# Decay attention and its FFN on one core: f loaded first, two scale loads in program order, FFN units dealt evenly per step

## The chip, the cores and the metric

The kernel runs on one core of one Trainium2 chip. The metric is the device time of one execution in microseconds; shown is the median of several runs. The profile is one more execution, taken by the hardware profiler. The engines are called by what they do: TensorE (PE in the profile, its weight loads PEld), VectorE (DVE), ScalarE (ACT), GpSimd (POOL) and SyncE (SP), which only issues DMAs.

## The reference

Eight batches of eight heads, 576 positions, head size 64. The attention has a decay: the logs of f are summed along the sequence, and the difference of the sums is added to the scores. The heads' outputs, side by side, are 4608 tokens of 512 numbers, and go through a feed-forward network (FFN) of 2048 hidden units. The weights come as 64-bit floats.

```python
scores = scale * np.matmul(q, k.transpose(0, 1, 3, 2))
log_f = np.log(np.clip(f, 0.0001, 1.0))
cum = np.cumsum(log_f, axis=-1)
decay = cum[:, :, :, None] - cum[:, :, None, :]
scores = np.where(causal, -1000000000.0, scores + decay)
attn = softmax(scores)                    # written out in the reference
x = (attn @ v).transpose(0, 2, 1, 3).reshape(B * S, H * D)
h = x @ w_in
g = np.where(h >= 1, h, np.where(h <= -1, 0.0, (h + 1) ** 2 / 4))
out = g @ w_out
```

## The kernel before

**Jobs and rounds.** The attention works in jobs. A job is a pair of heads (`hp`, 0 to 3) of a batch over a range of row tiles `r0` to `r1` (128 rows each; the fifth tile has 64 rows). Batch 0 is cut in two: jobs 0-3 do row tiles 0 and 1, jobs 4-7 tiles 2 to 4. From batch 1 on a job does all five: jobs 8-11 are batch 1, 12-15 batch 2, and so on to job 35. Four jobs with the same rows are a round; when its last pair has its values, the tokens of these rows are complete and the FFN can use them.

**Steps.** The loop over `p` (L737) writes out the work job by job as a list of steps: one per row tile (scores of the next tile, softmax of this one), and as second entry `finish`, which multiplies the weights of job `p - 1` with its values and, after the last pair, sets `tokens`. So the tokens of a round become known in the second step of the next round's first job. Scores use matrix products in 32 bits up to job 11 and split 16-bit ones from job 12; values are split from job 8.

**The FFN** is dealt in units. A unit is one chunk of 256 tokens by one of eight blocks of 256 hidden units: `moe_front` (first product, L637, into PSUM tile `ph`; then ScalarE and VectorE, L646 to L651, through tile `u`) and `moe_back` (second product, L665), which is written out one unit later. There are 18 chunks, so 144 units. Chunk 0 is done in three groups of blocks, since the weights come late: `weight_load` and `weight_split` read and convert the eight blocks during jobs 1 to 6 (`CONVERT`), mostly on VectorE.

**How units are dealt.** At the head of each job the loop works out a `quota` from the units that are ready by then: a share of one in four, three, two or one, by how many jobs are left until the next change of `tokens`. After each step it writes out units until the job's share for that step is reached. What is not dealt by the end of the loop follows after it.

**Scales.** The 16-bit splits need powers of two that fit the largest value of a batch. `value_scale(b)` (L244, L245) and `query_scale(b)` (L268, L269) read a batch's v, or q and k, once more, in 288 KB pieces into tiles `vm` (two of them), take maxima on VectorE, and `across` (L119, L129) brings them together over partitions with TensorE in PSUM tile `s`, of which there is one and which the scores use too. `value_scale(b)` is called while the job before batch `b` runs, `query_scale(b)` three jobs ahead, in the first row step: for batch 2 in job 9. The loads of these are issued by GpSimd, which also makes the decay rows (L474, L478) that the scores are added to.

**Order.** The program is traced in the order of the loop, and a scheduler then sets the order on each engine by running the program through a model of the chip: an instruction that is ready goes, the earlier in the program first. So an instruction that waits for nothing but a free tile can be placed far ahead of the place where the loop wrote it. On the chip each engine then works off its queue in that order. `decay_sums` (L140) loads f, takes logs and running sums, and writes them to DRAM, from where `load_decay` (L372) spreads a head's sums over all partitions.

Of the kernel before, what the change touches and what calls it, by code (L numbers as in the profile page):

```python
# [30 lines left out]
NQK = 12  # L31
# [14 lines left out]
def kernel(  # L46
# [20 lines left out]
    nc = tc.nc  # L67

    B, H, S, D = q.shape
# [67 lines left out]
    cum_d = dram.tile([B * H, S], F32, name="cum_d")  # L137
    cq8 = const.tile([P, NT5, B * H], F32, name="cq8")

    def decay_sums():  # L140
        fl = early
        nb = B * H
        nc.sync.dma_start(fl[0:nb, 0:S], f.rearrange("b h s -> (b h) s"))
        nc.vector.tensor_scalar(
            out=fl[0:nb, 0:S], in0=fl[0:nb, 0:S], scalar1=1e-4, scalar2=1.0, op0=ALU.max, op1=ALU.min
        )
        nc.scalar.activation(fl[0:nb, S:2 * S], fl[0:nb, 0:S], AF.Ln)
        nc.gpsimd.memset(fl[0:nb, 3 * S:4 * S], 0.0)
        cum = fl[0:nb, 2 * S:3 * S]
        nc.vector.tensor_tensor_scan(  # L150
            out=cum, data0=fl[0:nb, S:2 * S], data1=fl[0:nb, 3 * S:4 * S], initial=0.0, op0=ALU.add, op1=ALU.add
        )
        nc.sync.dma_start(cum_d, cum)
        pt = ps1.tile([P, 1024], F32, name="big")
        twice = fl[0:nb, 0:P]
        nc.vector.tensor_copy(
            twice.rearrange("p (a b) -> p a b", a=2), cum[:, FULL:S].unsqueeze(1).broadcast_to([nb, 2, 64])
        )
        for t in range(NT5):
            nc.tensor.transpose(  # L160
                pt[:, nb * t:nb * t + nb], cum[:, P * t:P * t + P] if t < LAST else twice, ident[0:nb, 0:nb]
            )
        nc.vector.tensor_scalar(
            out=cq8.rearrange("p t n -> p (t n)"), in0=pt[:, 0:NT5 * nb], scalar1=8.0, scalar2=None, op0=ALU.mult
        )
# [70 lines left out]
    def value_scale(b):  # L236
        m4 = tiny.tile([P, NPAIR], F32, name="m4", bufs=2)
        for i in range(NPAIR):
            if b:
                st = two.tile([P, S], F32, name="vm")  # L240
            else:
                st = stage[:, i * S:(i + 1) * S]
            part = v[b, 2 * i:2 * i + 2].rearrange("h s d -> (h s d)").rearrange("(p n) -> p n", p=P)
            (nc.gpsimd if b else nc.sync).dma_start(st, part)  # L244
            nc.vector.tensor_reduce(  # L245
                out=m4[:, i:i + 1], in_=st, axis=AX.X, op=ALU.max, apply_absolute_value=True
            )
        m1 = tiny.tile([P, 1], F32, name="m1", bufs=2)
        nc.vector.tensor_reduce(out=m1, in_=m4, axis=AX.X, op=ALU.max)
        m = mv[:, b:b + 1]  # L250
        across(m, m1)
        if b:
            nc.vector.tensor_tensor(out=m, in0=m, in1=mv[:, b - 1:b], op=ALU.max)
        scale_of(sv[:, b:b + 1], pv[:, b:b + 1], m)
# [6 lines left out]
    def query_scale(b):  # L261

        ms = tiny.tile([P, 2, NPAIR], F32, name="m8", bufs=2)
        for j, src in enumerate((q, k)):
            for i in range(NPAIR):
                st = two.tile([P, S], F32, name="vm")
                part = src[b, 2 * i:2 * i + 2].rearrange("h s d -> (h s d)").rearrange("(p n) -> p n", p=P)
                nc.gpsimd.dma_start(st, part)  # L268
                nc.vector.tensor_reduce(  # L269
                    out=ms[:, j, i:i + 1], in_=st, axis=AX.X, op=ALU.max, apply_absolute_value=True  # L270
                )
        m2 = tiny.tile([P, 2], F32, name="m2q", bufs=2)
        nc.vector.tensor_reduce(out=m2, in_=ms, axis=AX.X, op=ALU.max)
        mk = tiny.tile([P, 2], F32, name="mk", bufs=2)
        across(mk, m2)
        sc = sqk[:, :, b]
        scale_of(sc, mk, mk)
        nc.vector.tensor_scalar(
            out=nsig[:, b:b + 1], in0=sc[:, 0:1], scalar1=sc[:, 1:2], scalar2=-8.0, op0=ALU.mult, op1=ALU.mult
        )  # L280
        nc.vector.reciprocal(nalpha[:, b:b + 1], nsig[:, b:b + 1])
        nc.vector.tensor_scalar(
            out=cqs[b % 2], in0=cq8[:, :, b * H:(b + 1) * H], scalar1=nsig[:, b:b + 1], scalar2=-0.125,
            op0=ALU.mult, op1=ALU.mult,
        )
# [412 lines left out]
    done = 0  # L698
    tokens = 0
    nload = 0  # L700
    nw = 0

    def ready():
# [33 lines left out]
    for p in range(njobs + 1):  # L737
# [26 lines left out]
        if p > 0:  # L764
            wp = pairs[p - 1]

            def finish():
                nonlocal tokens
                (early_values if wp.p < NPE else values)(wp, xs[wp.b])
                if wp.hp == NPAIR - 1:  # L770
                    if wp.b and wp.r0 == 0:
                        join_scales(wp.b - 1)
                    tokens = wp.b * S + wp.s1

            steps.insert(1, finish)
        load_weights(LOADS.get(p, 0))
        blocks = CONVERT.get(p, 0)
        quota = -(-ready() // (NPAIR - (p + NPAIR - 1) % NPAIR))
        before, wbefore = done, nw
        for i, st in enumerate(steps):  # L780
            st()
            while nw - wbefore < blocks * (i + 1) // len(steps):
                weight_step()
            while ready() and done - before < quota * (i + 1) // len(steps):
                if units[done] not in bsc and nw < NB:
                    break
                moe_unit(*units[done])
# [36 lines left out]
```

## Time and profile before

| what | value |
|---|---|
| median of 3 runs | 1199.87 us (1199.61 to 1200.08) |
| the profiled execution's own time | 1195.69 us |
| its span, first to last instruction | 1193.9 us |
| mean granted TensorE clock | 0.951 |
| busy in the span: TensorE, VectorE, ScalarE, GpSimd | 89%, 68%, 65%, 40% |

How to read the rows: a row of instructions gives start, duration, engine, line of the kernel, operation, tiles written and read, and in brackets how long the engine had been idle before and what ended that. A row of the stages gives the stretch, its length, each engine's busy time and number of instructions (x), the mean granted clock of TensorE (PEclk), the share of the DMA engines' time and the rate. A row of waits gives who waited for whom, then the total in us, the number of waits and the longest. In a group's row stand shapes, count, busy time and the mean ns of one; an issue's row ends with the size in KB and the median us to landing. SPq and POOL rows of DMA_DIRECT2D are issues of transfers.

### The profile page before, as it was taken

Reading aid. Unit: us, or ns where it says so; the run is one execution under the profiler, and the core shown is the slowest. Engines: PE = TensorE matmul, PEld = TensorE weight load, DVE = VectorE, ACT = ScalarE, POOL = GpSimd, SP = SyncE. Lnnn points to the kernel's source line nnn. Section 1 sums busy time; section 2 is a strip of 40 time slices with the busy share of each in tenths; the row PEclk is TensorE's granted clock in tenths of the full one; section 3 lists DMA queues with packets and bytes.
Section 4 is the critical chain, followed back from the end, with each engine's and each line's share of the span. In section 5 each row is a group of like instructions: output and inputs, shape, how many; then the busy total and the mean of one; then the engine's idle time right before and its main releaser. Section 6 shows DMA issues by size and latency. Waiting matters only on the chain. (4 is left out here: it accounts for less than half of the span.)

```text
span 1193.9 us, 24608 instructions
## 1 busy us (share of the span) xinstructions
PE 1064.8 (89%) x8871; PEld 681.6 (57%) x8871; DVE 806.8 (68%) x2140; ACT 770.4 (65%) x1599; POOL 476.1 (40%) x811
## 2 busy tenths in 40 slices
PE   2566766998689899999999999999999999999998
PEld 1334443655356556655666665565566666677665
DVE  5979878777778777768656666777767866522222
ACT  2756555758567767777667666786777776644443
POOL 3588643534464544544432232454434444000000
PEclk9767888999789999999999999999999999999999
DMA  8797744689989977867665555777767773300000
GB/s 269 220 296 210 216 138 143 134 192 162 181 159 201 188 132 161 153 137 147 123 115 103 108 111 116 149 157 139 141 129 146 128 130 66 74 19 2 19 18 18
DMA packets 392537, 162.60 MB, mean 136 GB/s; under 512 B 370016, under 2 KB 371040, under 8 KB 392416
## 3 DMA queue, kind: packets, MB, share of 16 engines
q1 hardware_dynamic: 377312, 115.03, 49.4%
q0 software_dynamic: 9920, 36.58, 10.8%
q10 hardware_dynamic: 5184, 9.44, 2.3%
q8 instruction: 69, 1.13, 0.4%
q14 instruction: 52, 0.43, 0.1%
HBM read 89.80 MB, written 9.58 MB: 83 GB/s over the span
## 5 line engine op out<-in xcount | busy, mean ns | idle before, releaser
L637 PE MATMUL ph<-x,place 128*128 128x256 f16 (+3 forms) x4608 | 430.3, 248 | 10.1 <-DVE u L648 8.0
L665 PE MATMUL po<-place,g 128*128 128x512 f16 x1728 | 412.8, 382 | 4.1 <-ACT g L650 3.9
L637 PEld LDWEIGHTS <-place 128*128 128x128 f16 x4608 | 355.4, 99 | 85.4 <-issue 29.2
L474 POOL TENSOR_SCALAR sdr<-ck,nsig,cqs 128x128 f32<-128x128 f32 (+1 forms) x192 | 154.3, 808 | 297.7 <-DVE pr L575 278.5
L665 PEld LDWEIGHTS <-g 128*128 128x128 f16 x1728 | 162.3, 98 | 176.9 <-issue 8.3
L560 ACT ACTIVATE sdr<-sdr,nm 128x128 f32<-128x128 f32 (+1 forms) x240 | 132.6, 553 | 75.8 <-DVE nm L556 75.1
L648 DVE SCALAR_TENSOR_TENSOR u<-ph,z,u 128x512 f32<-128x512 f32 x136 | 101.5, 746 | 107.0 <-ACT u L647 106.7
L646 ACT ACTIVATE u<-ph,z 128x512 f32<-128x512 f32 x136 | 104.4, 768 | 80.0 <-PE ph L637 78.1
L650 ACT ACTIVATE g<-u,z 128x512 f16<-128x512 f32 x136 | 97.8, 719 | 71.0 <-DVE u L648 67.1
L575 DVE SCALAR_TENSOR_TENSOR pr<-sdr,rc,pr 128x128 f16<-128x128 f32 (+1 forms) x224 | 116.3, 555 | 39.9 <-ACT pr L574 37.7
L651 DVE SCALAR_TENSOR_TENSOR g<-u,z,g 128x512 f16<-128x512 f32 x136 | 104.2, 766 | 48.1 <-ACT g L650 47.6
L574 ACT ACTIVATE pr<-sdr,rc 128x128 f16<-128x128 f32 (+1 forms) x224 | 112.6, 550 | 18.9 <-ACT sdr L560 14.3
L556 DVE CUSTOM_DVE_ANT_0 sdr<-s,sdr,nalpha 128x128 f32<-128x128 f32 (+1 forms) x192 | 98.4, 546 | 26.5 <-PE s L466 16.2
L466 PE MATMUL s<-qkT 64*128 64x128 f16 (+5 forms) x704 | 88.3, 347 | 26.7 <-DVE nm L556 23.9
L595 PE MATMUL big<-pT,vs 128*64 128x64 f16 (+3 forms) x1008 | 83.8, 291 | 18.6 <-DMA pT<-pr 10.8
L647 ACT ACTIVATE u<-u 128x512 f32<-128x512 f32 x144 | 89.8, 624 | 2.5
L478 POOL TENSOR_SCALAR_AFFINE_SELECT sdr<-sdr 128x128 f32<-128x128 f32 x240 | 85.0, 363 | 7.8
L595 PEld LDWEIGHTS <-vs 128*64 128x64 f16 x1008 | 53.1, 113 | 51.6 <-issue 33.2
L474 POOL TENSOR_SCALAR sd<-ck,nsig,cqs 64x576 f32<-64x576 f32 x48 | 47.0, 980 | 78.9 <-DMA ck<-cum_d 60.5
L466 PEld LDWEIGHTS <-qkT 64*128 64x128 f16 (+1 forms) x864 | 32.8, 99 | 59.7 <-issue 46.1
L390 DVE SCALAR_TENSOR_TENSOR qs<-qk,sqk,qs 128x640 f16<-128x640 f32 x48 | 42.4, 910 | 30.8 <-ACT qs L389 30.8
L389 ACT ACTIVATE qs<-qk,sqk 128x640 f16<-128x640 f32 x48 | 37.3, 820 | 38.8 <-DMA qkT<-qs 33.2
(163 smaller groups left out, 1140.3 us busy)
## 6 DMA issues: line engine op xcount, KB each, us to landing
ck<-cum_d POOLq DMA_DIRECT2D x48, 288.0 KB, 4.5
out_dram<-ot ACTq DMA_DIRECT2D x36, 256.0 KB, 3.5
qk<-in_k_dram SPq DMA_DIRECT2D x64, 128.0 KB, 3.1
vm<-in_v_dram POOLq DMA_DIRECT2D x28, 288.0 KB, 3.5
v<-in_v_dram SPq DMA_DIRECT2D x56, 128.0 KB, 3.0
qk<-in_q_dram SPq DMA_DIRECT2D x56, 128.0 KB, 2.8
vm<-in_q_dram POOLq DMA_DIRECT2D x24, 288.0 KB, 3.4
vm<-in_k_dram POOLq DMA_DIRECT2D x24, 288.0 KB, 3.4
```

The source lines that it names most:

```text
L466: nc.tensor.matmul(outs[h][:, c0:c1], lhsT=x[rows], rhs=y[rows, c0:c1], start=(i == 0), stop=(i == len(terms) - 1),)
L474: nc.gpsimd.tensor_scalar(out=sd[p0:p1, 0:wid], in0=w.ck[h][p0:p1, 0:wid], scalar1=w.nsig if w.p < NQK else w.nsig[p0:p1], scalar2=w.cqs[p ...
L556: nc.vector.tensor_tensor_reduce(out=a, in0=sp, in1=a, scale=w.nalpha, scalar=BIG, op0=ALU.add, op1=ALU.min, accum_out=nm[:, i:i + 1],)
L560: nc.scalar.activation(a, a, AF.Exp, bias=nm[:, i:i + 1], scale=-1.0, accum_out=sm[:, i:i + 1])
L574: nc.scalar.activation(pr[:, :, 0, i, :], a, AF.Copy, scale=rc[:, i:i + 1])
L575: nc.vector.scalar_tensor_tensor(out=pr[:, :, 1, i, :], in0=a, scalar=rc[:, i:i + 1], in1=pr[:, :, 0, i, :], op0=ALU.mult, op1=ALU.subtract,)
L595: nc.tensor.matmul(av[64 * h:64 * h + 64, at + s0:at + s1], lhsT=w.vs[:, vl, h, t, :], rhs=w.pT[:, t, pl, h, s0:s1], start=(t == 0 and pi ...
L637: nc.tensor.matmul(ph[:, fi, a0:a1], lhsT=wi[fb][:, wl, t, fi * P:(fi + 1) * P], rhs=xs[b][:, t, xl, s0:s0 + a1 - a0], start=(fi == 0 and ...
L646: nc.scalar.activation(u, h, AF.Relu, scale=z.u[:, i:i + 1], bias=z.h[:, i:i + 1])
L648: nc.vector.scalar_tensor_tensor(out=u, in0=h, scalar=z.t[:, i:i + 1], in1=u, op0=ALU.max, op1=ALU.min)
L651: nc.vector.scalar_tensor_tensor(out=g[:, 1], in0=u, scalar=z.r[:, i:i + 1], in1=g[:, 0], op0=ALU.mult, op1=ALU.subtract)
L665: nc.tensor.matmul(po[ch][i], lhsT=g[:, gl, fi * TC + i * P:fi * TC + (i + 1) * P], rhs=wo[fb][:, wl, fi, :], start=(first and fi == 0 and ...
```

## The change

There are three edits. The load of f is traced ahead of everything else on its queue, before the first pair's q and k; it stood inside `decay_sums`, behind them. The loads of `value_scale(1)` (four) and of `query_scale(2)` (eight) are passed to `keep_in_program_order`, which puts each behind the instruction traced before it on GpSimd's queue; the loads of the other batches are left as they were. And `quota` is replaced by a plan: when a round is complete, `finish` notes the units done, the units ready, the number of steps so far and the number of steps until the next round is complete; after each step, units are due in proportion to the steps since then.

```diff
+    nc.sync.dma_start(early[0:B * H, 0:S], f.rearrange("b h s -> (b h) s"))
     def decay_sums():
         fl = early
         nb = B * H
-        nc.sync.dma_start(fl[0:nb, 0:S], f.rearrange("b h s -> (b h) s"))
...
-            (nc.gpsimd if b else nc.sync).dma_start(st, part)
+            load = (nc.gpsimd if b else nc.sync).dma_start(st, part)
+            if b == 1:
+                tc.keep_in_program_order(load)
...
-                nc.gpsimd.dma_start(st, part)
+                load = nc.gpsimd.dma_start(st, part)
+                if 4 * (b + 1) == NQK:
+                    tc.keep_in_program_order(load)
...
+    plan = [0, 0, 0, 1]
+    step_no = 0
...
                     tokens = wp.b * S + wp.s1
+                    to_come = sum(r1 - r0 + 1 for _, _, r0, r1 in jobs[p:p + NPAIR])
+                    plan[:] = [done, ready(), step_no, max(1, to_come)]
...
-        quota = -(-ready() // (NPAIR - (p + NPAIR - 1) % NPAIR))
-        before, wbefore = done, nw
+        wbefore = nw
         for i, st in enumerate(steps):
             st()
             while nw - wbefore < blocks * (i + 1) // len(steps):
                 weight_step()
-            while ready() and done - before < quota * (i + 1) // len(steps):
+            step_no += 1
+            due = plan[0] + -(-plan[1] * (step_no - plan[2]) // plan[3])
+            while ready() and done < due:
```

## The prediction

> **What bounds the kernel now.** I read the page's head and its slices first, then cut the span into stages with the windows view, because the mean over the span says nothing here.
>
> ```profile
> span 1193.9 us, 24608 instructions
> PEclk9767888999789999999999999999999999999999
> ```
>
> The slices are 29.8 us each: the granted TensorE clock is below full speed in the first ten, then it is full. The stages below are cut where ScalarE first evacuates the values of jobs 3, 7, 11, 15 and 35, the last job of each round (here the first and the last of these five instructions):
>
> ```profile
> 88.77 0.45 ACT L536 ACTIVATE x<-po,sv 128x256 f16<-128x256 f32 x1
> 1042.09 0.65 ACT L604 ACTIVATE x<-big 128x576 f16<-128x576 f32 x1 [4.41 <-PE big L595]
> ```
>
> Busy time of all engines by stage:
>
> ```profile
> core 0: us, PE busy (x) PEld busy (x) DVE busy (x) ACT busy (x) POOL busy (x), PEclk, DMA share, GB/s
> 0.00:88.80 88.80, 41.35 (x175) 26.41 (x177) 64.20 (x186) 46.61 (x125) 52.71 (x89) 0.79 0.86 261
> 88.80:222.20 133.40, 95.04 (x566) 62.38 (x567) 108.91 (x313) 76.83 (x180) 76.98 (x116) 0.83 0.60 177
> 222.20:329.00 106.80, 91.90 (x669) 54.43 (x668) 81.15 (x233) 71.95 (x157) 46.83 (x88) 0.92 0.86 168
> 329.00:437.50 108.50, 95.38 (x906) 62.22 (x904) 83.38 (x221) 74.36 (x158) 54.59 (x98) 0.94 0.87 175
> 437.50:1042.10 604.60, 593.86 (x5371) 375.73 (x5371) 426.33 (x1134) 435.62 (x893) 245.03 (x423) 1.00 0.67 127
> 1042.10:1194.00 151.90, 147.22 (x1194) 100.41 (x1192) 42.81 (x57) 65.03 (x93) 0.00 (x0) 1.00 0.04 15
> ```
>
> From 437.5 us on TensorE is the bound: it idles 10.7 us in 604.6, and 4.7 in the last 151.9. Before that it idles 47.5, 38.4, 14.9 and 13.1 us. A unit moved from one late place to another is worth nothing; a unit moved from the end into an idle place early is worth up to its whole TensorE time.
>
> How many FFN units ran in each stage is read from the back half's matmuls (L665, twelve to a unit):
>
> ```profile
> 0.00:88.80 88.80, 0.00 (x0) 0.79 0.86 261
> 88.80:222.20 133.40, 17.03 (x60) 0.83 0.60 177
> 222.20:329.00 106.80, 32.17 (x132) 0.92 0.86 168
> 329.00:437.50 108.50, 31.05 (x133) 0.94 0.87 175
> 437.50:1042.10 604.60, 250.09 (x1056) 1.00 0.67 127
> 1042.10:1194.00 151.90, 82.44 (x348) 1.00 0.04 15
> ```
>
> That is 0, 5, 11, 11, 88 and 29 units. In the last stage nothing but units is left, so a unit costs 151.9 / 29 = 5.24 us of TensorE.
>
> **The dealing, part by part.** Before, tokens that become ready in job 4, 8, 12 ... were dealt over the next four jobs, so jobs 5-8 had 2 units each, 9-12 2, 13-16 4, 17-20 4, 21-24 6, 25-36 4, and 24 were left. The new plan starts inside the step that completes the round and counts its steps (16 for the cut batch, 24 for the others): jobs 4-7 get 2 each, 8-11 2, 12-15 4, 16-19 4, 20-23 6, 24-35 4, and 24 are left. Everything moves one job earlier. With the back half one unit late, the stages would have 0, 7, 8, 16, 88 and 25 units: changes of 0, +2, -3, +5, 0, -4. The gate on converted weights holds nothing up: three blocks are split by the end of job 3 and eight by the end of job 6, ahead of units 0 and 6 in jobs 4 and 7. The stages are costed one by one.
>
> Last stage: -4 x 5.24 = **-21.0 us**. It has no other work, so nothing can give that back inside it.
>
> Stage 437-1042: the same 88 units, **0**.
>
> Stage 329-437: five more units are 26.2 us of TensorE. It has 13.1 us of idle, and at the granted 0.94 some 0.06 x 95 = 5.7 us are lost to the clock. If both were filled the cost would be 26.2 - 18.8 = 7; if neither, 26. TensorE is 88% busy in it, nearer to filled; I take half the sum of both idle kinds plus a little for order, **+13** (7 to 26).
>
> Stage 222-329: three units fewer, -15.7 if TensorE set its length throughout. Against that stands the scale of batch 2, below, which I put at +11: **-5** net (-16 to +20).
>
> Stage 88-222: two units more. TensorE has 38.4 us idle; VectorE pays two instructions of a unit:
>
> ```profile
> L651 DVE SCALAR_TENSOR_TENSOR g<-u,z,g 128x512 f16<-128x512 f32 x136 | 104.2, 766 | 48.1 <-ACT g L650 47.6
> L648 DVE SCALAR_TENSOR_TENSOR u<-ph,z,u 128x512 f32<-128x512 f32 x136 | 101.5, 746 | 107.0 <-ACT u L647 106.7
> ```
>
> so 2 x 1.5 = 3 us on an engine that is 82% busy there. The units also take turns in PSUM tile `ph` and tile `u` with the row turning and the weight split. I take +2 for both, at most +8.
>
> **The loads in program order.** Today the scale loads run far ahead of their place, since they need only a free `vm` tile. Reduces of such loads (L269 queries and keys, L245 values) in the two early stages:
>
> ```profile
> 0.00:88.80 88.80, 4.41 (x6) 0.79 0.86 261
> 88.80:222.20 133.40, 19.33 (x26) 0.83 0.60 177
> 88.80:222.20 133.40, 11.99 (x16) 0.83 0.60 177
> ```
>
> The twelve pinned loads belong to batch 1's values (asked for in job 7) and batch 2's queries and keys (job 9). Would the loads behind them simply run ahead in their place? The trace says that tiles of one name are handed out in program order: batch 1's value maximum was ready early, and its transpose, which needs PSUM tile `s`, still came at its place in the program, though `s` had stood free in between:
>
> ```profile
> 22.65 0.15 DVE L249 TENSOR_REDUCE m<-m 128x1 f32<-128x4 f32 x1
> 198.67 0.37 PE L119 MATMUL s<-ident,m 128*1 128x128 f32 x1 [6.27 <-DVE nm L556]
> ```
>
> So all 76 queue behind job 7. In the first stage go four reduces of batch 1 and six of batch 2, ten of 0.74 us = 7.4 us of VectorE, and the waits on GpSimd's queue (the waits view to 222.2 us, and the longest one):
>
> ```profile
> POOL vm L268 <- DVE m L269: 18.9, 9, 8.3
> POOL vm L244 <- DVE m L245: 13.0, 5, 8.6
> 37.20 0.57 POOL L268 DMA_DIRECT2D vm<-in_q_dram  x1 [8.29 <-DVE m L269]
> 37.85 1.96 POOL L474 TENSOR_SCALAR pr<-ck,cq 128x128 f32<-128x128 f32 x2
> ```
>
> A load that waits for a tile blocks the decay row (L474) behind it, and scores wait for that row. The 8.6 us one lies before 22 us, where decay rows wait anyway (below). Bounds: 0, if VectorE's weight split fills what is freed, and -10; I take **-4**, about the half of the 7.4.
>
> [...] These rows show GpSimd slowed without any load:
>
> ```profile
> 39.91 0.95 POOL L474 TENSOR_SCALAR sdr<-ck,cq 128x128 f32<-128x128 f32 x2
> 46.45 6.30 POOL L474 TENSOR_SCALAR sdr<-ck,cq 128x128 f32<-128x128 f32 x2 [1.18 <-DMA ck<-cum_d]
> ```
>
> [...]
>
> In stage 88-222 up to 38 of the 42 reduces leave (28 us of VectorE of 108.9), with their 42 issues on GpSimd. What is late next is the chain score - decay - exponent - turn, which VectorE does not set alone. I take -6 (bounds 0 and -20, some three quarters of what leaves); with the units **-4** (-18 to +8). They come back after 222 us, where VectorE is 76 and 77% busy in two stages and idles 50.8 us together: room for 28 us, so I cost that at nothing; if the cover failed, the cost would stand in the third and fourth stage.
>
> Batch 2's scale is the added wait. Its eight loads now start when GpSimd reaches job 9, two tiles at a time. Its transpose stands in `s` ahead of job 9's third score row:
>
> ```profile
> vm<-in_q_dram POOLq DMA_DIRECT2D x24, 288.0 KB, 3.4
> 242.51 0.27 PE L119 MATMUL s<-ident,m2q 128*2 128x128 f32 x1
> 253.50 0.92 PE L466 MATMUL s<-qkT 64*128 64x384 f32 x4
> 18.53 0.55 POOL L268 DMA_DIRECT2D vm<-in_q_dram  x1 [4.12 <-DVE pv L107]
> 84.18 0.57 POOL L268 DMA_DIRECT2D vm<-in_k_dram  x1
> ```
>
> Four rounds of issue, landing and reduce are 4 x (0.57 + 3.4 + 0.74) = 19 us at best; GpSimd runs about a step ahead, which I put at 8 us as an estimate (two of the some 4 us steps of a 22 us job). So +11, with units as filler. At the pace of today's run ahead (first to last issue 65.7 us) it would be far more. Batch 1's values, two rounds, come in job 7, where GpSimd has eight row tiles to run ahead in: nothing.
>
> **f first.** Four issues on the SP queue precede f:
>
> ```profile
> 0.75 0.97 SPq L362 DMA_DIRECT2D qk<-in_q_dram  x2
> 1.77 0.97 SPq L362 DMA_DIRECT2D qk<-in_k_dram  x2
> 2.79 0.57 SPq L143 DMA_DIRECT2D x<-in_f_dram  x1
> 7.59 0.45 DVE L144 TENSOR_SCALAR x<-x 64x576 f32<-64x576 f32 x1 [7.59 <-DMA x<-in_f_dram]
> 22.42 1.61 POOL L474 TENSOR_SCALAR sdr<-ck,cq 128x128 f32<-128x128 f32 x3 [3.34 <-DMA ck<-cum_d]
> ```
>
> f goes 2.04 us earlier, and with it the logs, the sums, their trip through DRAM and the first decay rows, which end a wait at 22.42. The q and k loads go back by 0.57 us each behind it, with time to spare. Between 0 and -2.0; the whole start hangs on it: **-1.5**.
>
> **Sum:** -1.5 - 4 - 4 - 5 + 13 + 0 - 21 = -22.5 us on a profiled execution of 1195.7 us (span 1193.9). The median of the runs, 1199.87, is 4 us above it with the same program, so the forecast is 1199.9 - 22.5 = **1177.4**.
>
> **The rivals.** *Slower: batch 2's scale comes late.* The eight loads are served as slowly as today, when one waited behind the weight split and units; the third score row of job 9 waits up to 66 - 8 = 58 us instead of 11, of which some 12 us more are filled by units that are already due. That is +35: 1212. The gain is cancelled where the wait is some 34 us longer than I took. For it: the pace above, and that `s` is a single tile. Against: these reduces then stand first in the program, so they are not pushed back.
>
> *Units only change places.* The fourth stage takes the full +26, the early stages nothing (0, +2), f -1.5, the third stage -5: sum about 0, some 1200. For it: the clock of 0.94 and 88% busy. Against: 38.4 us of idle right where units go now.
>
> *The early stages give more.* If VectorE does set the pace from 30 to 222 us, the first gives -10 and the second -16 with its units: 1159. For it: 82% busy in order, plus queue waits. [...]
>
> **How the numbers follow.** My forecast 0.50, units only change places 0.16, early stages give more 0.19, late scale 0.15. The range takes in most of these: 1152 to 1206. A change of 0.2% (2.4 us) is about what a measurement of this kernel can tell. Faster: 0.50 + 0.19 + half of 0.16 + 0.01 = 0.78; same 0.05; slower 0.17.
>
> **What would show it.** Right: f's first reader near 5.5 us; no `vm` load before some 170 us; job 3's values evacuated near 83 us, job 7's near 212; a back half near 95-100 us; 25 units after job 35; about 131 us of last stage. Wrong: `vm` loads of batch 2's values at the start; third score row of job 9 more than 30 us behind the second with TensorE idle; a fourth stage of 130 us or more; VectorE above 95% between 222 and 437.

## The result and the profile after

| | before | after |
|---|---|---|
| median of 6 runs | 1199.74 us | 1228.38 us (1221.99 to 1233.86) |
| ratio, 95% interval | | 1.0254 [1.0213, 1.0295] |
| the profiled execution, span | 1193.9 us | 1220.2 us (own time 1221.99) |

The change makes the kernel 2.5% slower; the forecast was 1177.4 and faster. All line numbers of the attention and the FFN are five higher than before (scores L471, back half L670, row products L600, decay rows L479), those of the scale loads one to five (values L245 and their reduce L248, queries and keys L271 and L274). The profiled execution is the fastest of the six. Medians are of all runs; the ratios leave out executions more than 1.5% above the kernel's fastest, which are two of four in the run with three `vm` tiles, one of four in the one with all loads pinned, and one of ten (2783.68 us) in the one with f, both pins and the early query call.

The windows view of after, cut at the same five events (the values of jobs 3, 7, 11, 15, 35):

```profile
core 0: us, PE busy (x) PEld busy (x) DVE busy (x) ACT busy (x) POOL busy (x), PEclk, DMA share, GB/s
0.00:68.50 68.50, 40.40 (x171) 25.98 (x171) 46.67 (x143) 40.68 (x112) 40.72 (x67) 1.00 0.83 251
68.50:206.80 138.30, 105.46 (x628) 68.09 (x629) 97.87 (x306) 84.88 (x193) 62.09 (x86) 0.84 0.36 105
206.80:345.80 139.00, 91.72 (x620) 53.26 (x619) 102.00 (x271) 72.14 (x160) 67.64 (x127) 0.82 0.90 199
345.80:478.80 133.00, 115.22 (x1020) 72.92 (x1020) 100.13 (x246) 80.20 (x164) 61.08 (x108) 0.94 0.90 183
478.80:1087.90 609.10, 593.85 (x5389) 378.96 (x5388) 427.30 (x1129) 436.97 (x893) 244.54 (x423) 1.00 0.67 126
1087.90:1220.20 132.30, 127.44 (x1049) 87.08 (x1049) 36.73 (x49) 56.50 (x81) 0.00 (x0) 1.00 0.05 17
```

Stage by stage against before: -20.3, +4.9, **+32.2**, **+24.5**, +4.5, -19.5; sum +26.3, the difference of the spans. Job 7's values are done 15.4 us earlier, at 206.8 instead of 222.2. Then 56.7 us are lost in two stages, more than the shorter end gives back. In the third stage TensorE is busy as long as before (91.72 against 91.90) although it does two units fewer: it idles 47 us instead of 15, and its granted clock is 0.82 instead of 0.92.

The same cut for the back half's matmuls (L670, twelve to a unit), stages two to four and the last:

```profile
68.50:206.80 138.30, 22.24 (x84) 0.84 0.36 105
206.80:345.80 139.00, 27.17 (x108) 0.82 0.90 199
345.80:478.80 133.00, 46.76 (x181) 0.94 0.90 183
1087.90:1220.20 132.30, 71.17 (x300) 1.00 0.05 17
```

That is 7, 9, 15 and 25 units (before 5, 11, 11 and 29): the dealing does what it says. The loads do so in part. The first is issued at 100.76 us (below), before job 4's values are evacuated at 103.71, and not in job 7: the pin ties a load to the one instruction traced before it, not to its job. But what stands behind batch 1's four loads waits for batch 2's place in job 9, and between 206.8 and 345.8 us the groups of tile `vm` hold 42 loads, where the stage had 12 reduces before. The rows: the first load on GpSimd's timeline, the groups of tile `vm` in the third stage, and the queue of these loads between 220 and 345 us in the DMA view, of after and then of before (packets, MB, share of the DMA engines' time):

```profile
100.76 1.27 POOL L245 DMA_DIRECT2D vm<-in_v_dram  x2
...
L271 POOL DMA_DIRECT2D vm<-in_q_dram x16: 538/556/592, 224.0 to 337.4; - x16
L271 POOL DMA_DIRECT2D vm<-in_k_dram x14: 538/556/592, 234.9 to 343.6; - x14
L245 POOL DMA_DIRECT2D vm<-in_v_dram x12: 538/538/592, 245.8 to 322.7; - x12
...
q0 software_dynamic: 3535, 13.05, 39.4%
```

```profile
q0 software_dynamic: 1360, 5.01, 15.1%
```

Job 9, where batch 2's queries and keys are now loaded, took 38.4 us before and takes 60.8. TensorE's timeline of after in it, with the first and the last of the eight loads on GpSimd's queue:

```profile
223.43 0.70 PE L471 MATMUL s<-qkT 64*128 64x256 f32 x4
223.97 1.13 POOL L271 DMA_DIRECT2D vm<-in_q_dram  x2
243.46 0.54 POOL L271 DMA_DIRECT2D vm<-in_k_dram  x1 [1.34 <-DVE m L274]
248.19 0.27 PE L119 MATMUL s<-ident,m2q 128*2 128x128 f32 x1
256.61 0.92 PE L471 MATMUL s<-qkT 64*128 64x384 f32 x4
```

and the second score row of that job before (the third, at 253.50, stands in the prediction):

```profile
238.42 0.70 PE L466 MATMUL s<-qkT 64*128 64x256 f32 x4
```

The third row comes 33.2 us after the second, before 15.1. From 223.97 to 248.19 the eight loads are issued, land, are reduced and transposed in the single tile `s`: 24 us. TensorE works on FFN units meanwhile (37.5 us busy from 220 to 260). What it lacks comes later, when the units of the round are used up and the rows of jobs 10 and 11 wait. The back half's matmuls in the third stage, cut where they end, of after and then of before:

```profile
206.80:280.00 73.20, 27.17 (x108) 0.98 0.77 183
280.00:345.80 65.80, 0.00 (x0) 0.64 1.04 216
```

```profile
222.20:310.00 87.80, 32.10 (x132) 0.98 0.83 159
310.00:329.00 19.00, 0.08 (x1) 0.65 1.03 209
```

The rest, which holds only some 24 matmuls of front halves in either kernel, is 65.8 us long instead of 19.0, and TensorE idles 37 us in it instead of 10.

### The profile page after: what moved, and what is told of

Same layout as the page of the kernel before. It is cut to its first block, busy times and chain, and to the rows that moved or that the text cites. A ratio compares the mean times of both kernels' runs of the same rounds, so it can differ in the third digit from the quotient of the medians.

```text
span 1220.2 us, 24606 instructions
## 1 busy us (share of the span) xinstructions
PE 1074.1 (88%) x8871; PEld 686.3 (56%) x8871; DVE 810.7 (66%) x2140; ACT 771.4 (63%) x1599; POOL 476.1 (39%) x811
## 3 DMA queue, kind: packets, MB, share of 16 engines
q0 software_dynamic: 9920, 36.58, 11.3%
## 5 line engine op out<-in xcount | busy, mean ns | idle before, releaser
L642 PE MATMUL ph<-x,place 128*128 128x256 f16 (+3 forms) x4608 | 430.8, 248 | 14.3 <-DVE u L653 10.0
L670 PE MATMUL po<-place,g 128*128 128x512 f16 x1728 | 417.9, 384 | 10.3 <-ACT g L655 7.7
L670 PEld LDWEIGHTS <-g 128*128 128x128 f16 x1728 | 162.4, 99 | 181.5 <-ACT g L655 11.3
L479 POOL TENSOR_SCALAR sdr<-ck,nsig,cqs 128x128 f32<-128x128 f32 (+1 forms) x192 | 152.7, 799 | 279.5 <-DVE pr L580 258.9
L655 ACT ACTIVATE g<-u,z 128x512 f16<-128x512 f32 x136 | 97.7, 718 | 88.8 <-DVE u L653 87.5
L580 DVE SCALAR_TENSOR_TENSOR pr<-sdr,rc,pr 128x128 f16<-128x128 f32 (+1 forms) x224 | 118.5, 562 | 35.9 <-ACT pr L579 33.2
L471 PE MATMUL s<-qkT 64*128 64x128 f16 (+5 forms) x704 | 92.2, 357 | 33.5 <-DVE nm L561 31.3
L600 PE MATMUL big<-pT,vs 128*64 128x64 f16 (+3 forms) x1008 | 84.9, 296 | 39.5 <-DMA pT<-pr 34.0
L561 DVE CUSTOM_DVE_ANT_0 sdr<-s,sdr,nalpha 128x128 f32<-128x128 f32 (+1 forms) x192 | 98.2, 545 | 18.1 <-PE s L471 15.4
L600 PEld LDWEIGHTS <-vs 128*64 128x64 f16 x1008 | 56.0, 115 | 76.2 <-issue 57.3
L483 POOL TENSOR_SCALAR_AFFINE_SELECT sdr<-sdr 128x128 f32<-128x128 f32 x240 | 88.0, 375 | 8.3
L479 POOL TENSOR_SCALAR sd<-ck,nsig,cqs 64x576 f32<-64x576 f32 x48 | 43.4, 904 | 92.8 <-DMA ck<-cum_d 76.0
L471 PEld LDWEIGHTS <-qkT 64*128 64x128 f16 (+1 forms) x864 | 32.5, 98 | 60.3 <-issue 46.6
L394 ACT ACTIVATE qs<-qk,sqk 128x640 f16<-128x640 f32 x48 | 37.1, 820 | 33.2 <-DMA qkT<-qs 31.4
```

Of the source, the lines that this page charges most:

```text
L471: nc.tensor.matmul(outs[h][:, c0:c1], lhsT=x[rows], rhs=y[rows, c0:c1], start=(i == 0), stop=(i == len(terms) - 1),)
L479: nc.gpsimd.tensor_scalar(out=sd[p0:p1, 0:wid], in0=w.ck[h][p0:p1, 0:wid], scalar1=w.nsig if w.p < NQK else w.nsig[p0:p1], scalar2=w.cqs[p ...
L561: nc.vector.tensor_tensor_reduce(out=a, in0=sp, in1=a, scale=w.nalpha, scalar=BIG, op0=ALU.add, op1=ALU.min, accum_out=nm[:, i:i + 1],)
L580: nc.vector.scalar_tensor_tensor(out=pr[:, :, 1, i, :], in0=a, scalar=rc[:, i:i + 1], in1=pr[:, :, 0, i, :], op0=ALU.mult, op1=ALU.subtract,)
L600: nc.tensor.matmul(av[64 * h:64 * h + 64, at + s0:at + s1], lhsT=w.vs[:, vl, h, t, :], rhs=w.pT[:, t, pl, h, s0:s1], start=(t == 0 and pi ...
L642: nc.tensor.matmul(ph[:, fi, a0:a1], lhsT=wi[fb][:, wl, t, fi * P:(fi + 1) * P], rhs=xs[b][:, t, xl, s0:s0 + a1 - a0], start=(fi == 0 and ...
```

## The experiments

Two theories stood at the start. *Lateness*: batch 2's scale, at its place in job 9, stops the rows of that job. *Drained units*: the units are dealt a job early, and jobs 9 to 11 stand without them. From the second group of runs on a third is weighed, *mass*: the 64 loads that used to run ahead fall behind the pins into stages three and four, and take VectorE and DMA time there. Beside them stands *dealing*: units moved into early stages cost there what they save at the end.

### One edit at a time

f first alone:

```diff
+    nc.sync.dma_start(early[0:B * H, 0:S], f.rearrange("b h s -> (b h) s"))
     def decay_sums():
...
-        nc.sync.dma_start(fl[0:nb, 0:S], f.rearrange("b h s -> (b h) s"))
```

> Only f is loaded first; loads and dealing as before. Both theories (late scale of batch 2; units drained a job early) expect the same: f's first reader 2 us earlier, the time between 1196 and 1200 us. If a mere new order costs tens of us, this run shows it: above 1210.

1191.74 us, ratio 0.9947 [0.9923, 0.9972]: faster by 0.5%. f's first reader goes from 7.59 to 3.45 us, and job 3's values come at 79.6 instead of 88.8. This is the fastest kernel of the study that leaves nothing out.

Both pins alone (the two `keep_in_program_order`, old dealing, f where it was):

> Only the twelve loads are pinned; f and the dealing as before. Late scale: job 9 is held by the transpose of batch 2's maxima, the stage from job 7's to job 11's values takes 120 to 135 us (106.8 before, 139.0 with the whole change), the first two stages are some 12 us shorter, the time 1200 to 1215 us. Drained units: the pins alone cost nothing, that stage takes 110 us at most and the time is some 1185 us.

1227.87 us, ratio 1.024 [1.021, 1.0271]: the size of the whole loss, and more than either expectation. Its windows, stages one to four:

```profile
0.00:71.40 71.40, 43.43 (x177) 26.94 (x177) 54.29 (x164) 44.70 (x120) 46.09 (x71) 0.88 0.88 255
71.40:193.40 122.00, 94.31 (x548) 63.03 (x548) 86.64 (x279) 77.19 (x178) 61.48 (x83) 0.82 0.38 110
193.40:341.30 147.90, 102.83 (x682) 59.87 (x684) 102.06 (x264) 72.96 (x158) 65.16 (x121) 0.82 0.90 188
341.30:471.60 130.30, 108.17 (x968) 66.77 (x967) 99.04 (x263) 78.65 (x167) 63.95 (x116) 0.92 0.95 188
```

The first two stages gain 28.8 us, the next two lose 62.9. VectorE's work in the two pairs: 173.1 us in 222.2 before (78%) against 140.9 in 193.4 here (73%); then 164.5 in 215.3 (76%) against 201.1 in 278.2 (72%). Some 32 us of VectorE work left the first pair and 37 came into the second, and its share of the time there did not rise. The third stage's units, dealt as before, are used up at 290 us here, and its last 51 us have none.

The new dealing alone (`plan` instead of `quota`, the rest as before):

> Only the new dealing; f and the loads as before. Late scale: nothing holds job 9, the stage from job 7 to job 11 takes 95 to 107 us, the next one 115 to 130, the last 131; the time 1185 to 1200 us. Drained units: the stage from job 7 to job 11 takes 125 us or more since its units are gone by job 9, the time 1215 us or more.

1210.22 us, ratio 1.0096 [1.0063, 1.0129]. Windows, stages two to four:

```profile
83.00:227.70 144.70, 103.67 (x621) 65.77 (x620) 114.19 (x320) 80.34 (x183) 79.55 (x116) 0.86 0.57 164
227.70:339.20 111.50, 87.34 (x620) 51.13 (x619) 79.97 (x235) 69.55 (x157) 52.77 (x99) 0.86 0.85 172
339.20:469.70 130.50, 116.69 (x1041) 74.21 (x1040) 90.41 (x237) 81.54 (x171) 54.51 (x93) 0.92 0.78 142
```

With two more units stage two is 11.3 us longer, with two fewer stage three is 4.7 us longer, not shorter, and with some four more stage four is 22 us longer: together +38 for the 19.5 us that the end gives back. The time lies between the two expectations.

By the ratios -0.53, +2.40 and +0.96 make +2.83%, and the whole is +2.54%: with these intervals of 0.2 to 0.4% each, the parts may add.

### Which pin, and what of it

The whole change without the pin on queries and keys:

```diff
-                if 4 * (b + 1) == NQK:
-                    tc.keep_in_program_order(load)
```

> The whole change without the pin on batch 2's queries and keys (its eight loads may run as soon as batch 1's four have their tiles). Late scale: the transpose stands ready before job 9, the stage from job 7 to job 11 takes 107 us at most, the time 1180 to 1198 us. Drained units: that stage stays at 130 us or more and the time at 1220 us or more.

1201.15 us, ratio 1.0027 [1.0, 1.0055]: 27 us of the 28.6 go with this one pin. Without it the loads behind run ahead again: the second stage holds 43 reduces instead of 4.

The whole change, with batch 2's queries and keys asked for in job 8, one job earlier:

```diff
-                if r == w.r0 and w.hp == 1 and w.b + 1 < B and p + 3 >= NQK:
+                if r == w.r0 and w.hp == (0 if w.b == 1 else 1) and w.b + 1 < B and p + 4 >= NQK:
```

> The whole change, but batch 2's query and key scale is asked for one job earlier (job 8, first row step, instead of job 9), its loads still pinned there. If the loss is that the loads come too late for the transpose that stands in front of job 9's third score row, then job 9 falls from 60.8 us to some 35 and the stage from job 7 to 11 from 139.0 to 110-122 us; the time 1200 to 1212 us. If the mass of 72 reduces behind job 7 is what costs, that stage stays above 130 and the time at 1222 or more.

1206.57 us, ratio 1.0067 [1.0045, 1.009]; job 9 takes 27.9 us. 22 us are won by the place of the call alone, but not by the eight loads alone: those queued behind them follow, and the second stage holds 25 reduces instead of 4. So neither run parts lateness from mass. (The profiled execution of the second, 1194.41 us, is the fastest of its five.) The third stages, without the pin and then with the earlier call:

```profile
223.00:335.90 112.90, 85.73 (x607) 49.55 (x607) 84.25 (x239) 68.14 (x154) 55.70 (x104) 0.88 0.94 194
```

```profile
218.20:330.60 112.40, 87.21 (x604) 49.44 (x605) 91.20 (x250) 69.43 (x153) 63.97 (x119) 0.88 1.04 223
```

Does lateness act through the single tile `s`? The whole change, with batch 2's maxima transposed in tile `ph`:

```diff
-        pt = ps1.tile([P, 2, 512], F32, name="s")[:, 0]
+        pt = ps.tile([P, 2, TC], F32, name="ph").rearrange("p f t -> p (f t)") if own else ps1.tile([P, 2, 512], F32, name="s")[:, 0]
...
-        across(mk, m2)
+        across(mk, m2, own=(b == 2))
```

> The whole change, loads as late as in it, but the transpose of batch 2's maxima takes a turn of PSUM tile ph instead of the single tile s. If holding s is what stops job 9, its third score row follows the second within 12 us (33 us in the change) and job 9 takes 45 us at most; the units, which use ph, then wait instead, and the time falls by 5 to 20 us. If job 9 waits for something else, it stays at 55 to 61 us.

1223.29 us, ratio 1.0203 [1.0164, 1.0241]. TensorE's timeline:

```profile
223.07 0.75 PE L471 MATMUL s<-qkT 64*128 64x256 f32 x4
225.77 1.20 PE L471 MATMUL s<-qkT 64*128 64x384 f32 x4 [1.96 <-DVE nm L561]
...
257.29 0.37 PE L119 MATMUL ph<-ident,m2q 128*2 128x128 f32 x1
```

The third row now comes 2.7 us after the second and job 9 takes 39.5 us instead of 60.8. The units last until 320 us, and only the stage's last 14 us have none. Yet only 5 us of the time are won: of the 21 us that job 9 gains, job 10 loses 8, and the fourth stage is 6 us longer. The hold of `s`, the mechanism of the prediction's slower rival, is there and is worth some 5 us, at the edge of what these intervals can tell.

Third stage with less work: the kernel before, with no units dealt in jobs 9 to 12:

```diff
+        if 9 <= p <= 12:
+            quota = 0
```

> The kernel before, but jobs 9 to 12 are dealt no units (they are added to jobs 13 to 16); nothing else is changed. If the attention's own chain sets the stage from job 7 to 11, it stays at 95 us or more of 106.8, although some seven units or 37 us of TensorE leave it. If TensorE sets it, it falls to 70-80 us.

1204.63 us in a single run. It tests nothing: its third stage still holds 132 back-half matmuls, the 11 units of before. The scheduler must have drawn them in from the places where the loop had left them.

Three tiles `vm` instead of two, in the whole change, so that more loads are under way:

```diff
-                st = two.tile([P, S], F32, name="vm")
+                st = two.tile([P, S], F32, name="vm", bufs=3)
```

> The whole change with three vm tiles instead of two, so that batch 2's eight loads need fewer rounds. If the lateness of these loads is the loss, the third score row of job 9 follows the second by some 22 to 27 us instead of 33, and the time falls by 4 to 12 us, to 1216-1224. If it is the reduces' mass or the order, it stays within 3 us of 1228.

1232.67 us (1217.17 to 1239.80), ratio 1.0212 [1.0142, 1.0281], which cannot be told from the change's 1.0254. In its profiled execution (1236.57 us) the eight loads and their transpose take 20.7 us instead of 24.2, and between 220 and 345 us the loads' queue takes 50.6% of the DMA engines instead of 39.4%. Whether more loads under way help a little stays open; they do not undo the loss.

All loads pinned, so that none gather behind the twelve:

```diff
-            if b == 1:
+            if b:
...
-                if 4 * (b + 1) == NQK:
+                if b:
```

> The whole change with the loads of every batch from 1 on kept at their places in program order, not those of two alone, so that loads of batches 2 to 7 cannot gather behind the pinned ones. Theory mass: the third stage's 42 loads fall to 20 or fewer, the pT landing to 3.5-4.5 us, the third stage to 115-128 us, the time to 1203-1217 (less if later stages gain, more if each later batch's scale is now late). Theory lateness alone: job 9 near 60 us, third stage 133-141, the time 1220-1232.

1274.25 us, ratio 1.059 [1.0525, 1.0655], the slowest of all and outside both expectations. In the profiled execution (1283.39 us, the slowest of the four) the third stage does shorten, to 125.9 us, as mass would have it; with 12 reduces, as many as before, it is still 19 us longer than before. But the long stage, 437 to 1042 before, takes 678.7 us instead of 604.6: 48 scale loads now stand in it, where there were none.

### Mass against lateness

To take the mass away and leave the lateness, the loads of queries and keys from batch 3 on and of values from batch 2 on were cut to 72 of 576 columns, which leaves seven eighths of those maxima out. The pinned loads stay whole. (The cut also shortens GpSimd's waits for a free `vm` tile: those that a maximum of q or k ends take 8.5 us instead of 13.1 in the changed kernel's third stage.)

```diff
-            load = (nc.gpsimd if b else nc.sync).dma_start(st, part)
+            load = (nc.gpsimd if b else nc.sync).dma_start(st[:, 0:S // 8] if b > 1 else st, part[:, 0:S // 8] if b > 1 else part)
...
-                load = nc.gpsimd.dma_start(st, part)
+                load = nc.gpsimd.dma_start(st[:, 0:S // 8] if b > 2 else st, part[:, 0:S // 8] if b > 2 else part)
...
-                    out=ms[:, j, i:i + 1], in_=st, axis=AX.X, op=ALU.max, apply_absolute_value=True
+                    out=ms[:, j, i:i + 1], in_=st[:, 0:S // 8] if b > 2 else st, axis=AX.X, op=ALU.max, apply_absolute_value=True
```

In the whole change:

> The whole change, but the scale loads of q and k for batches 3 and later and of v for batches 2 and later read 72 of 576 columns, and their maxima run over these (this leaves seven eighths of those maxima out). Batch 2's own loads of q and k, pinned, stay whole and as late as in the changed kernel. Theory mass (the held-back loads, all falling in the third stage, delay the transposes of the rows and take VectorE): the third stage goes from 139.0 us to 112-125, the median landing of pT transposes from 5.2 us to 3.5-4.5, the time to 1200-1215. Theory lateness alone (only batch 2's late scale and the single tile s cost): job 9 stays near 60 us, the third stage at 133-141, the time at 1218-1230.

1199.68 us, ratio 1.0001 [0.9981, 1.002], 28.7 us less than the changed kernel, with job 9 still at 54.4 us. By the expectation that is mass. But the cut may be worth that anywhere, and the control says so. The same cut in the kernel before, and in the kernel with both pins alone:

> The kernel before with the same cut: q, k loads of batches 3 and later and v loads of batches 2 and later read an eighth, maxima over that (seven eighths of those maxima left out). Control for the cut in the changed kernel, which took 28.7 us away. If that was the burst (the mass falling into one stage because the pins held it back), the kernel before, whose loads are spread, gains little: 1190-1198. If the loads cost the same wherever they stand, it gains as much: 1165-1175.

> Both pins alone, old dealing, f where it was, with the same cut. Without the cut the pins cost 28 us against before. If the mass of the held-back loads is the cost, the pins under the cut stand within 10 us of the kernel before under the cut, third stage 115-128 us (147.9 uncut): about 1198-1206. If lateness of batch 2's scale is the cost: the third stage stays above 138 us, and the pins still cost 20-28 us against before under the cut.

1168.82 us, ratio 0.9767 [0.9719, 0.9816], as the expectation has it if the loads cost the same wherever they stand, and 1184.99 us, ratio 0.9906 [0.9871, 0.9941], between its two expectations. And the whole change with the cut and with the transpose in `ph`:

> As the kernel with the cut loads (q, k of batches 3 and later, v of batches 2 and later read an eighth, which leaves that part of the maxima out), and batch 2's maxima are transposed in tile ph instead of s. If lateness and mass are the two halves of the pins' cost and nothing else is in it: job 9 at 30-40 us, the third stage 100-112, the time 1190-1202, near the whole change without the pin on q and k (1201). If there is a third cost in the pins: above 1206.

1194.83 us, ratio 0.9974 [0.9952, 0.9996]: by the medians 5 us less than with the cut alone, the same 5 as without it. The square:

| median us | loads whole | loads cut | the cut is worth, by the ratios to before in the same session |
|---|---|---|---|
| before | 1199.7 | 1168.8 | 28 |
| both pins | 1227.9 | 1185.0 | 40 |
| whole change | 1228.4 | 1199.7 | 30 |

The pins cost 2.4% with whole loads and 0.9906 / 0.9767 = 1.014, 1.4%, with cut ones. So of their 28 us some 12 go with the cut, which I call mass (with both intervals, 12 give or take 8), and some 16 stay. I call these lateness, though they hold all that the cut leaves, the pinned loads' own size and the new order among it. In the whole change the loss is 2.5% with whole loads and 1.0001 / 0.9767 = 1.024 with cut ones: there the mass costs nothing on balance that these runs can tell. What it cost in stages one to four it now costs in stages three and four. Stages two to four of the kernel before under the cut, then of the pins, then of the whole change:

```profile
87.20:205.50 118.30, 90.34 (x552) 58.84 (x552) 92.79 (x309) 75.22 (x175) 76.13 (x112) 0.84 0.39 103
205.50:304.80 99.30, 92.07 (x682) 54.23 (x684) 77.13 (x237) 72.45 (x159) 49.23 (x91) 0.97 0.82 158
304.80:410.30 105.50, 92.17 (x893) 59.67 (x894) 80.72 (x238) 75.17 (x163) 58.43 (x100) 0.95 0.85 154
```

```profile
72.30:195.20 122.90, 91.95 (x548) 61.26 (x548) 86.72 (x277) 77.29 (x178) 60.16 (x82) 0.81 0.37 109
195.20:325.20 130.00, 101.33 (x693) 58.57 (x692) 90.23 (x281) 75.05 (x163) 69.55 (x130) 0.87 0.79 148
325.20:432.60 107.40, 93.08 (x915) 60.59 (x912) 82.37 (x245) 74.48 (x162) 64.62 (x110) 0.98 0.90 155
```

```profile
68.50:208.40 139.90, 105.77 (x627) 67.88 (x628) 98.66 (x308) 85.03 (x192) 62.69 (x87) 0.84 0.36 104
208.40:333.10 124.70, 90.03 (x610) 53.25 (x611) 84.65 (x272) 69.62 (x153) 68.58 (x129) 0.84 0.77 153
333.10:456.80 123.70, 113.39 (x1046) 71.78 (x1047) 88.40 (x256) 83.81 (x174) 62.96 (x111) 0.96 0.74 135
```

Read down the third stage: 99.3, 130.0, 124.7. With almost no mass the pins still add 30.7 us to it, 24.5 of them in job 9 (30.1 to 54.6), where the third score row comes 40 us after the second instead of 13.5. That part is lateness. Read across the second: the cut takes 15.1 us from before (133.4 to 118.3), nothing from the pins (122.0 and 122.9), so early loads were not free where they ran ahead. And the dealing, with f, costs 1.0% between the last two kernels (0.9906 to 1.0001) and 0.1% between the uncut pair (1.024 to 1.0254), where the two edits alone would make 0.4%. It may be that a kernel which already waits in the third and fourth stage covers the dealing's price; with intervals of 0.2 to 0.4% on each ratio that is not shown.

### Looking for a better version

f and the pin on batch 1's values, old dealing; then f, both pins, the query call in job 8, old dealing:

> f first and batch 1's value loads pinned, dealing and batch 2's loads as before: the two edits that cost nothing so far. If the edits add up as the runs suggest (f -6, value pin -3, pin on queries and keys +27, dealing +12), 1188 to 1193 us, level with or ahead of f alone (1191.7). If the value pin by itself brings the late loads that the pin on queries and keys brings, 1200 or more.

> f first, both pins, batch 2's scale asked for at job 8, and the dealing of before. By the theory of the late transpose: the first two stages as with the pins alone (193 us in all, 222 before), the third some 110-118, the fourth 110-125: 1180 to 1198 us, ahead of the kernel before. If the moved reduces cost by their mass, the third and fourth stage take 270 us together as with the pins alone and the time is 1215 or more.

1208.41 us, ratio 1.0107 [1.0062, 1.0152], and 1213.04 us, ratio 1.0105 [1.0068, 1.0141]. The first meets the worse of its two expectations, the second lies between the two. The value pin alone already holds back every later load, since `vm` tiles are handed out in program order (batch 2's first load comes at 115.78 us, right behind batch 1's four): 17 us worse than f alone. Batch 2's scale is on time there, its eight loads issued by 136.6 us, and the third stage takes 131.3 us all the same. So a long third stage is not by itself the mark of a late scale, and this kernel's loss stays unexplained. With the new dealing in addition, it is the kernel without the query pin, at 1201.15: there the dealing gains 7 us, where alone it costs 11.

Dealing the first round by the plan alone, and the whole plan with its first round begun four steps later:

```diff
...
+            due = before + quota * (i + 1) // len(steps)
+            if 4 <= p < 8:
+                due = plan[0] + -(-plan[1] * (step_no - plan[2]) // plan[3])
```

```diff
-                    plan[:] = [done, ready(), step_no, max(1, to_come)]
+                    plan[:] = [done, ready(), step_no + (4 if p == 4 else 0), max(1, to_come)]
```

> The kernel before, but with the first round's units dealt by the plan (jobs 4 to 7); every later round as before. If the dealing's cost is the units in jobs 4 to 7, stages two and three together take 250 to 258 us and the time is 1206 to 1213 us. If it lies in the later rounds, the time is 1196 to 1201 us.

> The new dealing alone, but the first round's units begin a job later (jobs 5 to 8, as before); from job 8 on as in the change. If the dealing's cost is the units in jobs 4 to 7, where units share tiles ph and u with the row turning and the weight split, stages two and three together are back at 240-247 us (256.2 with the dealing alone, 240.2 before) and the time is 1196 to 1203 us. If it lies in the later rounds, the time stays at 1207 or more.

1202.25 us, ratio 1.0041 [1.0016, 1.0067], and 1199.16 us, ratio 1.0013 [0.9989, 1.0038]. The early start of the first round, into jobs 4 to 7, is all of the dealing's loss when it is taken away, and not quite half of it when it is done alone (there stage two is 14.3 us longer and stage three, with two units fewer, 4.9 us shorter). What is left of the dealing, four units moved from the end to the fourth stage, gains nothing: the stage is 125.6 us instead of 108.5. Adding f to that:

> The kernel before with f first and the new dealing, the first round's units beginning a job later; no pins. If f's gain (8.0 us alone) and this dealing (-0.6 us alone) add: 1189-1194. If they share the same slack: 1195-1200, no better than f alone.

1198.27 us, ratio 0.9996 [0.9973, 1.002]. f's 0.5% is gone too: job 3's values come 6.2 us earlier, and the third stage is 10 us longer.

## Why the prediction was wrong

**Last stage, -21.0.** Right: 25 units, -19.5, still 132.3 / 25 = 5.29 us a unit.

**f first, -1.5.** Right in sign, too small: its first reader went 3.9 to 4.1 us earlier (3.70 in the changed kernel, forecast 5.5), and alone it is worth 0.5% of the time. I had taken only the issue slots, 2.04 us; from its issue to that reader the load also took 2.94 us in the changed kernel (0.76 to 3.70) instead of 4.80 (2.79 to 7.59), which gains nearly as much again.

**First stage, -4.** Mis-sized: job 3's values at 68.5 us, 20.3 earlier (forecast 83); the pins alone give 17.4. That a pair of decay rows took 6.30 us on GpSimd where another took 0.95, without any load, spoke for a term of 0; the pins' stage, 71.4 us instead of 88.8, does not bear that out. So the early loads, or the order that came with them, did set its pace; whether by their waits on GpSimd's queue or by VectorE's 7.4 us, no run separates. The pinned loads did not keep to job 7 either: the first came at 100.76 us, where the prediction named some 170.

**Stage 88-222, -4.** +4.9. The loads' part was taken at -6 and is -11.4 in the pins alone; the units' part was taken at +2 and is +11.3 in the dealing alone. Here I argued from 38.4 us of idle TensorE: the units had room on the engine, and the stage grew all the same. They share `ph`, `u` and VectorE with the row turning and the weight split, which is the likely reason; no run isolates it.

**Stage 222-329, -5.** This is where it fell: +32.2. Two steps failed. The first is "+11" for batch 2's scale. The four rounds were forecast at 19 us and took 24.2 from the first issue to the transpose (223.97 to 248.19), and the head start of 8 us did not exist: the first load was issued 0.5 us after the second score row. The third row came 18.1 us later than before, where +11 was forecast, and job 9 took 22.4 us longer. Then the filler was gone: the units that covered the wait were missing in jobs 10 and 11, where the stage stood 65.8 us without a back half. Pins alone add 41.1 us to the stage, and 30.7 with the loads behind them cut. Nor did the row gap tell the price, since taking away the hold of `s` won some 5 us. The pin's place decides (27 us without it, 22 a job earlier), and with it the place of all that stands behind it; how the two make up the price beyond the square above is open. The second is -15.7 for three units fewer. Two left the stage, 10.5 us of work, and the dealing alone lengthened it by 4.7 us (the plan in the first round alone shortened it by 4.9). TensorE did not set its length throughout, which the term had as its condition.

**Loads that come back after 222 us, "at nothing".** Failed for the pins: 12 us or so, by the square. The 50.8 us of idle VectorE that were to hold them were no full cover. VectorE stood between 68 and 82% in the first four stages of the kernels shown here, with the loads and without; the pins' third and fourth stage grew by 62.9 us when 37 us of its work came there. Half of that growth, 32.6 us, stays with the loads cut. I had named that condition ("if the cover failed, the cost would stand in the third and fourth stage") and gave it no share of the range.

**Stage 329-437, +13.** +24.5, within the 7 to 26 given, at its upper end, with four units more instead of five. In the dealing alone four cost 22 us there, their whole TensorE time; with the first round begun later, 17. But the pins alone, with the old dealing, lengthen the stage by 21.8 too, so that the hit is in part luck. **Stage 437-1042, 0.** +4.5.

Of the rivals, the late scale was the nearest (1212, given 0.15), with the right place. It had neither the units' price nor the loads' beside it; and *units only change places* was right for the fourth stage (+26 there, +22 in the dealing alone), not for the early ones, which it put at 0 and +2. I had treated them as alternatives, and they came together. Of the four signs named for "wrong", a fourth stage of 133 us came, and a row gap of 33 us, but with TensorE busy in it. VectorE stood at 73 and 75%, not at 95. Of those for "right", the first back half (94.97 us), the 25 units and the last stage came. One reading was short: the slices of the clock show 7 and 8 once more in the eleventh and twelfth, so that it is full from some 358 us on and not from 298; no term hangs on it.

What stays open: whether the mass acts by VectorE's time, by the DMA engines or by GpSimd's waits for tiles, since the cut took from all three (34 us of reduces, 16.5 MB). In the changed kernel TensorE waits longer for transposes of the weights in the third stage (these rows are after, then before). But the waits from 280 us on fall where no units are left to cover them, and with the transpose in `ph` and the same loads the row shows 1.3 us, for a time only 5 us shorter:

```profile
PE big L600 <- DMA pT<-pr: 21.4, 7, 8.8
```

```profile
PE big L595 <- DMA pT<-pr: 2.9, 3, 2.3
```

Open is also why the value pin costs 17 us beside f with no scale late, and why the dealing gains 7 us beside that pin and costs 11 alone. Each edit makes the scheduler set a new order on all engines, and the runs show the sums only.

## What to carry to other kernels

Idle time of an engine in a stage is not yet room for its work: two more units made a stage with 38.4 us of idle TensorE 11.3 us longer. Before sending work into such idle time, double or halve some work of that kind there and see what the stage does. Work that covers a wait is missing afterwards; count what is left of it for the next one. A load that runs far ahead of its place may look like disorder, and be the reason that its consumer never waits; if it is pinned, pin it early enough for its users, and count everything that queues behind it for the same tiles. When one edit removes a cost and moves work, run the same removal in the kernel before as well: the cut here looked like the proof of the mass theory until the control gained the same 28 us.

## What the hardware showed that was not expected

The granted TensorE clock went with the units within one stage: 0.98 in the part of the third stage that holds the back halves, before and after, and 0.65 and 0.64 in the rest without them, where TensorE was busy 9.1 of 19.0 us and 28.7 of 65.8. So the stage's mean fell from 0.92 to 0.82 as the rest grew, and 91.7 us of busy time were kept while two units, 2 x 5.24 = 10.5 us of work by the last stage before, at 1.00, had left: a 128x512 product of the weights took 551 ns in the stage instead of 449, and 390 in the long stage before, at 1.00. A busy share alone does not give the clock: the first stage before had 0.79, with TensorE busy 47% of it, and in it the first 30 us had 1.00 at 24% busy, the last 28.8 us 0.59 at 61%; the first stage of the new dealing alone had 1.00 at 52% (42.80 of 83.00 us). A busy sum of TensorE is thus no measure of its work where the clock differs.

A load of 288 KB and its 0.75 us reduce cost some half a microsecond of the whole time each: 64 loads cut to an eighth gave 28 us in the kernel before, where they stood in all of the first 437 us, 30 in the changed one, and 40 with the pins alone.
